# VectorE's score blocks as a fourth concurrent row tile, conversions in pairs, and new planner rules, in an attention kernel with two softmax engines

## The chip, the cores and the metric

The kernel runs on one core of one Trainium2 chip. The metric is the device time of one execution in microseconds (us); lower is better. One execution of each kernel was profiled, the others were timed. Where a ratio is given, it is the mean time of one kernel's fast runs over that of the kernel before in the same rounds on the same chip, so it is not quite the ratio of the medians quoted beside it. "Fast" means within 1.5% of the fastest run of the same kernel; a run above that is called slow.

## The reference

Two independent attention blocks with 2048 positions, 512 channels, 32 heads of 16 channels each; the results lie side by side.

```python
def _A_ref(x, wqkv, wo):        # linear attention, cut
    pq, pk = phi(q), phi(k)     # phi(t) = where(t > 0, t + 1, exp(t)) + 1e-6
    kv = einsum("bhsd,bhse->bhde", pk, v); z = einsum("bhsd->bhd", pk)
    o = einsum("bhqd,bhde->bhqe", pq, kv) / (einsum("bhqd,bhd->bhq", pq, z) + 1e-6)
    return o @ wo
def _B_ref(x, wqkv, wo):        # softmax attention, cut
    p = softmax(einsum("bhqd,bhkd->bhqk", q, k) * 16 ** -0.5)
    return einsum("bhqk,bhkd->bhqd", p, v) @ wo
```

The softmax block dominates: 32 heads of 2048 x 2048 exponentials. The kernel cuts it into 2048 *blocks*, each of 128 keys and 512 queries of one head; 64 blocks (4 heads, all keys, the same 512 queries) make a *unit*.

## The kernel before

ScalarE takes most blocks by its exponential. VectorE takes the rest with an integer trick: one conversion of the scores to int16 out of PSUM (`DI`), then a *chain* of four cheap operations over a group of blocks. TensorE makes the scores (32 rows of the array per block) and multiplies the results with the values.

A planner writes the program: it keeps a clock `T` for each engine, asks each source of work for its next candidate, and takes the earliest. Its estimates only fix the order of instructions; semaphores fix the real times. So **any edit of a rule gives another program**.

The kernel uses eight banks of PSUM: five for ScalarE's scores (fills of 3 and of 2 blocks in turn), one accumulator `PVb` for the value products of one unit, and two spare banks `DB`. VectorE's scores share the spare banks with all other work: projections, the whole linear attention, the output.

```python
ABL = (3, 2); DG = 3; NDG = 5; DNEXT = 16           # fills; blocks per chain group; groups; see fill_d_cand
DI = sb("DI", [128, NDG, DG * 512], I16)
DQ = sb("DQ", [128, 2, DG * 512], I16)              # temporaries of the chain
PVb = ps("pPV", [128, 512], F32)
DB = [ps("pD%d" % i, [128, 512], F32) for i in range(2)]

def qk(e, dst, b):                                  # scores of one block: 32 rows of the array, row group g
    u, j, g = b
    Gp, c, e_ = unit(u)
    return e.matmul(dst, lhsT=KM[32*g:32*g+32, Gp % 2, e_, j*128:(j+1)*128],
                    rhs=QT[32*g:32*g+32, Gp % 2, c*512:(c+1)*512], start=True, stop=True, tile_position=(32*g, 0))

def fill_act_cand():                                # ScalarE's fill: 3 or 2 blocks in different row groups
    ...
    def f(e):
        for i, b in enumerate(bl):
            ins = qk(e, SCR[sl][:, i*512:(i+1)*512], b)
        return ins
    sch.add("pe", f, reads=qk_reads(bl), writes=skeys(sl))

def fill_d_cand():                                  # VectorE's block: a TensorE item of its own
    ...
    elif left[u] < DNEXT:                           # near the end of a unit: take from the next one
        u += 1
    ...
    sch.add("pe", lambda e: qk(e, f32v(bk), bl[0]), reads=qk_reads(bl), writes=[bk[3]])
    ... e.tensor_scalar(DI[:, buf, i*512:(i+1)*512], f32v(bk), ESC, EB, op0=ALU.mult, op1=ALU.add)
```

The value product of a unit must be complete before the next unit may start in `PVb`. ("Head" and "head's end": a unit and its end.)

## Time and profile before

| | before |
|---|---|
| time, median of 4 runs | 879.28 us (876.78 to 881.74) |
| span of the profiled run | 877.5 us |
| blocks on ScalarE / VectorE | 1699 / 349 |
| ScalarE idle between its first and last exponential | 58.2 us |
| of that in stretches over 1 us | 34.8 us in 10 stretches |

The last two rows are counted from the trace (0.2 us more than before the exponentials alone, as some idle time lies before other instructions).

The first parts of the page of the kernel before follow. The first line of numbers has the busy time of each engine. The rows of digits are ScalarE's busy share in tenths in 40 equal slices of the span; PEclk is the clock that TensorE was granted, in tenths of full speed.

```profile
span 877.5 us, 12952 instructions
...
PE 756.4 (86%) x5361; PEld 225.4 (26%) x5406; DVE 733.2 (84%) x1245; ACT 799.5 (91%) x737; POOL 45.9 (5%) x43
...
ACT  6999989999999999999897997999889889999793
...
PEclk9989989999999989878776798978897879687777
```

ScalarE is the busiest engine, and the late slices of PEclk are much lower than the early ones. Next, groups by line and shape of the kernel before: engine, operation, tile written and read, shapes, count, then busy time, mean ns of one, and the idle time of the engine just before them, with what ended it.

```profile
L726 ACT ACTIVATE PT<-pS 128x1536 f16<-128x1536 f32 x340 | 526.2, 1548 | 37.8 <-PE pS L662 36.4 <-PE pD L662 0.6
L726 ACT ACTIVATE PT<-pS 128x1024 f16<-128x1024 f32 x339 | 380.1, 1121 | 20.2 <-PE pS L662 17.8 <-PE pD L662 1.8
L777 DVE TENSOR_SCALAR DI<-pD 128x512 int16<-128x512 f32 x349 | 230.3, 683 | 34.7 <-PE pD L662 26.0 <-PE pS L662 7.1
...
L662 PE MATMUL pD<-QT,KM 32*128 32x512 bf16 x349 | 133.4, 432 | 16.2 <-DVE DI L777 7.9 <-DVE VNa L545 2.7 <-DVE PQT L535 2.1
...
L816 DVE TENSOR_TENSOR DQ<-DQ 128x1536 bf16<-128x1536 int16 x116 | 109.9, 951 | 1.0
```

The exponentials cost 788.0 us together, or 788.0 / 1699 = 0.464 us a block. The 58 us of idle time before them ended almost always with a score matmul: ScalarE starves for scores. A VectorE block costs 0.68 us for the conversion and a third of the chain.

In ten-microsecond windows of the kernel before, three places look like this (busy time and count of each engine, then the granted clock, DMA share and GB/s).

```profile
core 0: us, PE busy (x) PEld busy (x) DVE busy (x) ACT busy (x) POOL busy (x), PEclk, DMA share, GB/s
520.00:530.00 10.00, 6.26 (x28) 2.03 (x29) 9.73 (x16) 4.81 (x5) 1.03 (x1) 0.79 0.00 0
630.00:640.00 10.00, 7.27 (x43) 2.01 (x43) 9.53 (x17) 4.91 (x5) 0.00 (x0) 0.58 0.05 15
810.00:820.00 10.00, 5.32 (x24) 1.61 (x21) 9.51 (x15) 5.33 (x5) 0.00 (x0) 0.50 0.00 0
```

ScalarE loses half of each window and VectorE is the busy one. TensorE pauses, and its granted clock is low there.

### The profile page before, as it was taken

Reading aid. Unit: us, or ns where it says so; the run is one execution under the profiler, and the core shown is the slowest. Engines: PE = TensorE matmul, PEld = TensorE weight load, DVE = VectorE, ACT = ScalarE, POOL = GpSimd, SP = SyncE. Lnnn points to the kernel's source line nnn. Section 1 sums busy time; section 2 is a strip of 40 time slices with the busy share of each in tenths; the row PEclk is TensorE's granted clock in tenths of the full one; section 3 lists DMA queues with packets and bytes.
Section 4 is the critical chain, followed back from the end, with each engine's and each line's share of the span. In section 5 each row is a group of like instructions: output and inputs, shape, how many; then the busy total and the mean of one; then the engine's idle time right before and its main releaser. Section 6 shows DMA issues by size and latency. Waiting matters only on the chain.

```text
span 877.5 us, 12952 instructions
## 1 busy us (share of the span) xinstructions
PE 756.4 (86%) x5361; PEld 225.4 (26%) x5406; DVE 733.2 (84%) x1245; ACT 799.5 (91%) x737; POOL 45.9 (5%) x43
## 2 busy tenths in 40 slices
PE   8989889988888889888988878899689889888776
PEld 5323323223222222212222122222122222221212
DVE  5796665898889978899989999799998998979882
ACT  6999989999999999999897997999889889999793
POOL 2000021100000022100000012200000000000000
PEclk9989989999999989878776798978897879687777
DMA  9001000000000000000000000000000000000000
GB/s 313 24 2 49 1 1 1 1 2 1 1 1 1 1 1 1 1 13 7 7 1 6 8 7 7 1 7 7 6 7 1 7 7 31 7 25 1 7 19 27
DMA packets 13137, 13.48 MB, mean 15 GB/s; under 512 B 1808, under 2 KB 12560, under 8 KB 13072
## 3 DMA queue, kind: packets, MB, share of 16 engines
q1 hardware_dynamic: 12272, 12.19, 4.3%
q8 instruction: 44, 0.72, 0.3%
q10 hardware_dynamic: 800, 0.39, 0.2%
q14 instruction: 21, 0.17, 0.1%
HBM read 8.39 MB, written 4.19 MB: 14 GB/s over the span
## 4 chain that ended last, share of the span: by engine, by line
ACT 55%; PE 24%; DVE 19%; issue 1%; POOL 0%; ACTq 0%; POOLq 0%
ACT PT L726 54%; PE pPV L872 8%; DVE DI L777 7%; PE pS L662 7%; DVE DI L818 3%; DVE DQ L816 3%; PE pD L662 3%; DVE DQ L817 1%; DVE DQ L815 1%; PE pD L896 1%; PE pD L448 1%; ACT EA L532 1%; PE pD L613 1%; PE pD L604 1%; DVE OT L893 1%
## 5 line engine op out<-in xcount | busy, mean ns | idle before, releaser
L726 ACT ACTIVATE PT<-pS 128x1536 f16<-128x1536 f32 (+1 forms) x680 | 788.0, 1334 | 58.0 <-PE pS L662 54.2
L662 PE MATMUL pS<-QT,KM 32*128 32x512 bf16 x1699 | 295.6, 430 | 65.9 <-ACT PT L726 59.9
L777 DVE TENSOR_SCALAR DI<-pD 128x512 int16<-128x512 f32 x349 | 230.3, 683 | 34.7 <-PE pD L662 26.0
L872 PE MATMUL pPV<-PT,VV 128*17 128x512 f16 x1699 | 213.3, 437 | 2.9 <-DVE OT L893 1.7
L662 PE MATMUL pD<-QT,KM 32*128 32x512 bf16 x349 | 133.4, 432 | 16.2 <-DVE DI L777 7.9
L662 PEld LDWEIGHTS pS<-QT,KM 32*128 32x128 bf16 x1699 | 65.3, 92 | 308.0 <-ACT PT L726 260.6
L816 DVE TENSOR_TENSOR DQ<-DQ 128x1536 bf16<-128x1536 int16 (+1 forms) x117 | 110.3, 946 | 1.0
L818 DVE TENSOR_TENSOR DI<-DI,DQ 128x1536 int16<-128x1536 int16 (+1 forms) x117 | 110.0, 946 | 0.9
L872 PE MATMUL pPV<-DI,VV 128*17 128x512 f16 x349 | 86.5, 437 | 10.6 <-DVE DI L818 10.2
L474 POOL TENSOR_SCALAR KM<-KR,PAR 128x512 bf16<-128x512 bf16 x24 | 41.1, 1725 | 519.4 <-DVE KR L472 519.4
L815 DVE TENSOR_SCALAR DQ<-DI 128x1536 int16<-128x1536 int16 (+1 forms) x117 | 64.4, 557 | 0.7
L817 DVE TENSOR_SCALAR DQ<-DQ 128x1536 f16<-128x1536 bf16 (+1 forms) x117 | 64.4, 557 | 0.7
L872 PEld LDWEIGHTS pPV<-PT,VV 128*17 128x17 bf16 x1699 | 37.1, 89 | 91.7 <-issue 77.2
L662 PEld LDWEIGHTS pD<-QT,KM 32*128 32x128 bf16 x349 | 29.7, 93 | 90.0 <-DVE DI L777 41.2
L541 PE MATMUL pD<-Wa,xTa 128*128 128x256 bf16 x256 | 40.5, 288 | 0.9 <-DVE VNa L545 0.4
L448 PE MATMUL pD<-xTb,Wb 128*128 128x512 bf16 x103 | 34.0, 410 | 4.6 <-issue 2.1
L896 PE MATMUL pD<-identf,OT 128*128 128x128 f32 x128 | 30.4, 349 | 4.0 <-DVE OT L893 2.4
L893 DVE COPY OT<-pPV 128x512 f32<-128x512 f32 x32 | 21.9, 685 | 13.4 <-PE pPV L872 13.3
L417 DVE CAST OB<-pD 128x512 bf16<-128x512 f32 x30 | 20.6, 687 | 13.2 <-PE pD L613 13.0
L532 ACT ACTIVATE EA<-pD 128x256 bf16<-128x256 f32 (+1 forms) x48 | 28.0, 584 | 0.7 <-PE pD L541 0.7
L541 PEld LDWEIGHTS pD<-Wa,xTa 128*128 128x128 bf16 x256 | 21.2, 101 | 19.4 <-issue 10.5
L872 PEld LDWEIGHTS pPV<-DI,VV 128*17 128x17 bf16 x349 | 17.0, 91 | 35.3 <-DVE DI L818 17.4
(88 smaller groups left out, 378.9 us busy)
## 6 DMA issues: line engine op xcount, KB each, us to landing
out_dram<-OB SPq DMA_DIRECT2D x32, 128.0 KB, 1.7
KNa<-in_A_x_dram SPq DMA_DIRECT2D x4, 512.0 KB, 6.2
ON<-in_B_x_dram SPq DMA_DIRECT2D x3, 512.0 KB, 7.5
Wa<-in_A_wqkv_dram SPq DMA_DIRECT2D x1, 1536.0 KB, 12.0
Wb<-in_B_wqkv_dram SPq DMA_DIRECT2D x2, 384.0 KB, 8.4
Wb<-in_B_wqkv_dram SPq DMA_DIRECT2D x1, 512.0 KB, 6.6
WOb<-in_B_wo_dram SPq DMA_DIRECT2D x1, 512.0 KB, 12.1
WOa<-in_A_wo_dram SPq DMA_DIRECT2D x1, 512.0 KB, 12.2
```

The costliest lines, as they stand in the source:

```text
L448: return e.matmul(f32v(bk), lhsT=Wb[:, cc, kind * 512 + Gp * 128:kind * 512 + Gp * 128 + 128], rhs=xTb[:, cc, sc * 512:(sc + 1) * 512], st ...
L474: st.append(("pool", 0.7, f_op("pool", lambda e, e_=e_: e.tensor_scalar(KM[:, r, e_, cs], KR[:, kr, :], PAR[:, e_:e_ + 1], None, op0=ALU.m ...
L541: return e.matmul(f32v(bk)[:, 256 * k_:256 * k_ + 256], lhsT=xTa[:, cc, t * 128:(t + 1) * 128], rhs=Wa[:, cc, 512 + 512 * k_ + 256 * hp:51 ...
L662: return e.matmul(dst, lhsT=KM[32 * g:32 * g + 32, Gp % 2, e_, j * 128:(j + 1) * 128], rhs=QT[32 * g:32 * g + 32, Gp % 2, c * 512:(c + 1) ...
L726: sch.add("act", lambda e: e.activation(PT[:, row, c0:c0 + w], SCR[sl][:, 0:w], ACTF.Exp, scale=SC), reads=skeys(sl), writes=[("PT", row, ...
L777: sch.add("dve", lambda e: e.tensor_scalar(DI[:, buf, i * 512:(i + 1) * 512], f32v(bk), ESC, EB, op0=ALU.mult, op1=ALU.add), reads=[bk[3]] ...
L815: (0.07 + w * 0.00027, lambda e: e.tensor_scalar(Dq, I, 0x200, 6, op0=ALU.bitwise_xor, op1=ALU.logical_shift_left), ik, [("DQ", q)]),
L816: (0.07 + w * 0.00053, lambda e: e.tensor_tensor(Dqb, Dq, Dq, op=ALU.mult), [("DQ", q)], [("DQ", q)]),
L817: (0.07 + w * 0.00027, lambda e: e.tensor_scalar(Dqh, Dqb, EC, EO, op0=ALU.mult, op1=ALU.add), [("DQ", q)], [("DQ", q)]),
L818: (0.07 + w * 0.00053, lambda e: e.tensor_tensor(I, I, Dqh, op=ALU.add), ik + [("DQ", q)], ik)]
L872: sch.add("pe", lambda e, g=g, j=j, h=h, P=P, first=first, last_=last_: e.matmul(PVb[32 * g:32 * g + 17, 0:512], lhsT=VV[:, j, vcol(h):vco ...
L896: return e.transpose(f32v(bk)[:, qb * 128:(qb + 1) * 128], OT[:, ob, qb * 128:(qb + 1) * 128], identf[:])
```

## The change

Its intent: a fill of 3 uses three of the four row groups of the array, so a VectorE block can ride along as the fourth, and TensorE no longer spends a separate slot on it. Two VectorE blocks that lie in both spare banks are converted by one operation. Along with it come new rules for the planner.

```diff
-    DG = 3
-    NDG = 5
+    DG = 4
+    NDG = 4
-    DNEXT = 16
+    DNEXT = 24
+    DLEAD = 0.5
+    DBL = 5.0
-        DQ = sb("DQ", [128, 2, DG * 512], I16)
+        DQ = sb("DQ", [128, 1, DG * 512], I16)
-        DB = [ps("pD%d" % i, [128, 512], F32) for i in range(2)]
+        DB = ps("pD", [128, 1024], F32)
 ...
+        def d_pick(at, used):
+            bi = min((i for i in range(2) if dfree[i] is not None), key=lambda i: (dfree[i], i), default=None)
+            u = cur_unit()
+            if bi is None or u is None or dfree[bi] > at or d_backlog(at) > DBL:   # bank free now; backlog under 5 us
+                return None
 ...
+        def d_emit(tk, en):
+            for b, buf, bi, i in tk:
+                bk = DBANK[bi]
+                sch.add("pe", lambda e, bk=bk, b=b: qk(e, f32v(bk), b), reads=qk_reads([b]), writes=[bk[3]])
+            pair = len(tk) == 2 and tk[0][1] == tk[1][1] and tk[0][2] == 0 and tk[1][2] == 1
 ...
+                    sch.add("dve", lambda e: e.tensor_scalar(DI[:, buf, i * 512:(i + n) * 512], DB[:, bi * 512:(bi + n) * 512],
+                                                             ESC, EB, op0=ALU.mult, op1=ALU.add),
 ...  in fill_act_cand:
+                tk = []
+                while len(bl) + len(tk) < 4:
+                    pk = d_pick(st + 0.05, [g for _, _, g in bl] + [x[0][2] for x in tk])
+                    if pk is None:
+                        break
+                    tk.append(d_take(pk))
                 sch.add("pe", f, reads=qk_reads(bl), writes=skeys(sl))
+                if tk:
+                    tk.sort(key=lambda x: x[3])
+                    d_emit(tk, en + 0.05)
 ...  fill_d_cand stays for blocks alone, with the same rules
```

`d_backlog` is VectorE's planned work ahead plus 1 us for each block whose chain has not been scheduled. I call `DBL` the *cap* and `DNEXT` the *head limit*. `DLEAD`: a block alone is planned no earlier than 0.5 us before VectorE's planned work runs out.

More of the change, by code (lines that the diff above doesn't have):

```diff
@@ L296, in bass_concat_heads__linear_attn_block__softmax_full_mha__prompt_kernel @@
         PVb = ps("pPV", [128, 512], F32)
-        DB = [ps("pD%d" % i, [128, 512], F32) for i in range(2)]
+        DB = ps("pD", [128, 1024], F32)
         def bank(T, b0, key):
             return (T, T.bitcast(BF), b0 * 512, key)
-        DBANK = [bank(DB[i], 0, ("D", i)) for i in range(2)]
+        DBANK = [bank(DB, i, ("D", i)) for i in range(2)]
         SBANKS = [bank(SCR[i], b, ("S", i, b)) for i in range(2) for b in range(ABL[i])]
@@ L677, in bass_concat_heads__linear_attn_block__softmax_full_mha__prompt_kernel @@
         ptfree = {}
-        dgroup = {"n": 0, "buf": 0, "items": [], "open": False}
+        dgroup = {"n": 0, "buf": 0, "open": False}
         dgfree = [0.0] * NDG
         dgleft = [0] * NDG
-        qfree, qwait = [0, 1], []
+        qfree, qwait = [0], []
         def cur_unit():
@@ L687, in cur_unit, with d_backlog @@
             return None
+        def d_backlog(at):
+            w = max(0.0, T["dve"] - at) + sum(c_[3] for c_ in cands["dve"])
+            for s_ in dgroup["st"].values():
+                if not s_.get("chained"):
+                    w += 1.0 * len(s_["items"])
+            return w
+        def d_pick(at, used):
[3 more added lines that the diff above has]
+                return None
+            if u == NU - 1:
+                if left[u] < DEND:
+                    return None
+            elif left[u] < DNEXT:
+                u += 1
+            if not dgroup["open"]:
+                buf = dgroup["n"] % NDG
+                if dgfree[buf] is None or dgfree[buf] > at:
+                    return None
+            else:
+                buf = dgroup["buf"]
+            ch = choose(u, 1, used)
+            if ch is None or not ch[0] or ch[1] > at:
+                return None
+            return ch[0][0], buf, bi
@@ new lines, in d_take @@
+        def d_take(pk):
+            b, buf, bi = pk
+            take([b])
+            dfree[bi] = None
+            if not dgroup["open"]:
+                dgroup.update(open=True, buf=buf)
+                dgroup["n"] += 1
+                dgfree[buf] = None
+                dgleft[buf] = 0
+                dgroup["st"][buf] = {"p1": 0, "closed": False, "items": []}
+            s_ = dgroup["st"][buf]
+            i = len(s_["items"])
+            s_["items"].append(b)
+            dgleft[buf] += 1
+            if len(s_["items"]) == DG:
+                s_["closed"] = True
+                dgroup["open"] = False
+            return b, buf, bi, i
@@ new lines, in d_emit, with p1 @@
+        def d_emit(tk, en):
[3 more added lines that the diff above has]
+            pair = len(tk) == 2 and tk[0][1] == tk[1][1] and tk[0][2] == 0 and tk[1][2] == 1
+            for part in ([tk] if pair else [[x] for x in tk]):
+                n = len(part)
+                _, buf, bi, i = part[0]
+                def p1(st_, en_, part=part, n=n, buf=buf, bi=bi, i=i):
+                    sch.add("dve", lambda e: e.tensor_scalar(DI[:, buf, i * 512:(i + n) * 512], DB[:, bi * 512:(bi + n) * 512],
+                                                             ESC, EB, op0=ALU.mult, op1=ALU.add),
+                            reads=[("D", bi + x) for x in range(n)], writes=[("DI", buf, i + x) for x in range(n)])
+                    for x in range(n):
+                        dfree[bi + x] = en_ + LAT
+                    s_ = dgroup["st"][buf]
+                    s_["p1"] += n
+                    s_["t"] = en_
+                    chain(buf)
+                push("dve", en + LAT, 0, 0.1 + 0.55 * n, p1)
@@ L689, in fill_act_cand @@
+        dgroup["st"] = {}
         def fill_act_cand():
@@ L719, in run @@
                 sch.add("pe", f, reads=qk_reads(bl), writes=skeys(sl))
+                if tk:
+                    tk.sort(key=lambda x: x[3])
+                    d_emit(tk, en + 0.05)
+                    T["pe"] = en + 0.05
                 w = 512 * len(bl)
@@ L734, in fill_d_cand @@
         def fill_d_cand():
-            bi = min((i for i in range(2) if dfree[i] is not None), key=lambda i: dfree[i], default=None)
-            if bi is None:
-                return None
-            u = cur_unit()
-            if u is None:
-                return None
-            if u == NU - 1:
-                if left[u] < DEND:
-                    return None
-            elif left[u] < DNEXT:
-                u += 1
-            if not dgroup["open"]:
-                buf = dgroup["n"] % NDG
-                if dgfree[buf] is None:
-                    return None
-                t1 = dgfree[buf]
-            else:
-                buf, t1 = dgroup["buf"], 0.0
@@ L753, in fill_d_cand @@
-            ch = choose(u, 1)
-            if ch is None or not ch[0]:
-                return None
-            bl, t0 = ch
-            start = max(T["pe"], t0, t1, dfree[bi])
-            def run(st, en):
-                take(bl)
-                dfree[bi] = None
-                if not dgroup["open"]:
-                    dgroup.update(open=True, buf=buf, items=[])
-                    dgroup["n"] += 1
-                    dgfree[buf] = None
-                    dgleft[buf] = 0
-                i = len(dgroup["items"])
-                items = dgroup["items"]
-                items.append(bl[0])
-                dgleft[buf] += 1
-                state = dgroup.setdefault("st", {})
-                state.setdefault(buf, {"p1": 0, "closed": False})
-                if i == 0:
-                    state[buf] = {"p1": 0, "closed": False, "items": items}
-                bk = DBANK[bi]
-                sch.add("pe", lambda e: qk(e, f32v(bk), bl[0]), reads=qk_reads(bl), writes=[bk[3]])
-                def p1(st_, en_):
-                    sch.add("dve", lambda e: e.tensor_scalar(DI[:, buf, i * 512:(i + 1) * 512], f32v(bk), ESC, EB, op0=ALU.mult, op1=ALU.add),
-                            reads=[bk[3]], writes=[("DI", buf, i)])
-                    dfree[bi] = en_ + LAT
-                    state[buf]["p1"] += 1
-                    state[buf]["t"] = en_
-                    chain(buf)
-                push("dve", en + LAT, 0, 0.62, p1)
-                if len(items) == DG:
-                    state[buf]["closed"] = True
-                    dgroup["open"] = False
@@ L787, in fill_d_cand @@
-            return start, 0.3, run
+            fr = [x for x in dfree if x is not None]
+            if not fr:
+                return None
+            busy = max(T["dve"], T["pe"]) if not cands["dve"] else max(T["dve"], T["pe"]) + sum(c_[3] for c_ in cands["dve"] if c_[0] < T["dve"] + 1.0)
+            at = max(T["pe"], min(fr), busy - DLEAD)
+            if dgroup["open"] is False and dgfree[dgroup["n"] % NDG] is not None:
+                at = max(at, dgfree[dgroup["n"] % NDG])
+            at = max(at, T["pe"] + d_backlog(T["pe"]) - DBL + 0.01)
@@ L789, in close_group @@
+            pk = d_pick(at + 1e-6, ())
+            if pk is None:
+                return None
+            def run(st, en):
+                tk = [d_take(pk)]
+                pk2 = d_pick(st + 0.05, [tk[0][0][2]])
+                if pk2 is not None:
+                    tk.append(d_take(pk2))
+                tk.sort(key=lambda x: x[3])
+                d_emit(tk, en)
+            return at, 0.32, run
         def close_group():
@@ L798, in chain @@
                 return
+            s_["chained"] = True
             qwait.append(buf)
@@ L1083, in bass_concat_heads__linear_attn_block__softmax_full_mha__prompt_kernel @@
             S=S, NT=NT, NC=NC, vcol=vcol, xTb=xTb, Wb=Wb, WOb=WOb, VV=VV, QT=QT, KM=KM, PT=PT, ON=ON, OT=OT, ZR=ZR, ONT=ONT, OB=OB,
-            identb=identb, identf=identf, BMk=BMk, SCR=SCR, PVb=PVb, MB=DB[0], GM=OT[:, 0, 0:2 * NT].rearrange("p (a t) -> p a t", a=2), GT=RD[0:NT, 0, :], out=out), gsems)
+            identb=identb, identf=identf, BMk=BMk, SCR=SCR, PVb=PVb, MB=DB, GM=OT[:, 0, 0:2 * NT].rearrange("p (a t) -> p a t", a=2), GT=RD[0:NT, 0, :], out=out), gsems)
         totals = {}
```

## The prediction

> **What bounds it now.** By the page's first part, ScalarE is busy 799.5 us of 877.5 (91%), TensorE 756.4, VectorE 733.2. By the groups by form, ScalarE's exponentials are 340 of 3 blocks (1548 ns each) and 339 of 2 (1121 ns): 788.0 us for 1699 of the 2048 score blocks, 0.464 us a block. VectorE does the other 349. In the chain of waits ScalarE holds 55%, TensorE 24%, VectorE 19%: ScalarE sets the pace, but is starved. Idle before the exponentials is 58.0 us, 54.2 of it for the score matmuls. The timeline around 470-480 us shows a typical loss: value matmuls wait 1.4 us for a late VectorE block of a head (the single accumulator bank can't go on to the next head), TensorE's granted clock is 0.60, and ScalarE is busy 5.6 of 10 us. In ten-microsecond windows the same happens at 520, 630, 710 and 810 us (ScalarE 4.8, 4.9, 6.3, 5.3). Another 10 us at the start and 14 at the end have none.
>
> **What changes.**
> 1. TensorE. The 349 VectorE score matmuls often run alone (timeline, 466-472 us), with ScalarE's next fill behind them in order. The Trainium skill (TensorE: Matmul & The Clock Gate, Packing small matmuls) says matmuls in different row groups overlap; this trace agrees: bursts of 2 or 3 take the 0.39 us of one. As fourth tile (or third and fourth beside a two-block fill) a block should cost almost nothing. Estimate: about 0.2 us for each of some 250-300 blocks, 50-60 us of TensorE time, not all critical.
> 2. VectorE. A 512-wide conversion takes 683 ns. The skill (VectorE: DVE Perf Modes, errata table) gives PSUM-source time as a constant plus one cycle per element at 0.96 GHz, so estimate 533 ns + 150 fixed, and 1216 ns for 1024: 75 ns saved per block of a pair. The trace confirms 683 only. The chain's four operations per three blocks take 559+951+559+951 = 3020 ns; for four I estimate 3.8 us, 0.95 against 1.01 a block. Together 1.69 to about 1.56-1.60: 30-45 us.
> 3. The planner can give VectorE more blocks: I expect 370-410 instead of 349, 10-28 us less ScalarE work (0.464 each).
> 4. VectorE blocks go to the next head from 24 blocks left, not 16, and VectorE's backlog is capped at 5 us. Both should make the late VectorE block at a head's end rarer.
> 5. Against: a pair takes both spare banks at once, which projections and output jobs share; the groups of four close later; one temporary instead of two; fewer separate matmuls may let the granted clock (0.866) fall.
>
> **Sum.** Exponentials about 770 (1660 blocks), other ScalarE 11 in the main stretch, start and end 26, leaving idle: 58 now, perhaps 35-40 after. That is about 845.
>
> **Predicted:** 847 us, 8 in 10 between 825 and 873. Faster by over 2%: 0.74; within 2%: 0.20; slower: 0.06.
>
> **Signs.** The conversion group shows 1024-wide forms near 1.2 us, most blocks in pairs; score matmuls to the VectorE banks start within nanoseconds of a fill's, with less waiting for VectorE before them; idle before the exponentials under 45 us; exponential blocks below 1680; TensorE busy under 720 us.
>
> **What would make it wrong.** If the idle before exponentials does not fall, the stalls are from latency at a head's end or the clock, not TensorE work. If VectorE's blocks fall below 340, the cap bites and ScalarE gains work. If pairs are rare, the VectorE gain is missing. If jobs starve for banks, the end without exponentials grows.

## More of the kernel before

Where does it starve? This timeline of the kernel before (start, length, engine, line, operation; idle time and its end in brackets) shows the costliest kind of place, a head's end.

```profile
632.14 0.68 DVE L777 TENSOR_SCALAR DI<-pD 128x512 int16<-128x512 f32 x1
...
633.61 0.95 DVE L818 TENSOR_TENSOR DI<-DI,DQ 128x1536 int16<-128x1536 int16 x1
634.61 0.60 PE L872 MATMUL pPV<-DI,VV 128*17 128x512 f16 x3 [2.40 <-DVE DI L818]
...
635.41 0.68 DVE L893 COPY OT<-pPV 128x512 f32<-128x512 f32 x1
...
638.46 0.60 PE L662 MATMUL pS<-QT,KM 32*128 32x512 bf16 x5
...
638.90 1.45 ACT L726 ACTIVATE PT<-pS 128x1536 f16<-128x1536 f32 x1 [5.09 <-PE pS L662]
```

A VectorE block of the old head is converted at 632.14; its chain ends after 634.5; the value matmuls on `DI` have waited 2.40 us for it; only then can the accumulator be copied (L893) and the value products and scores of the next head follow. ScalarE had sat idle for 5.09 us at 638.90.

The clock records of the trace say which came first: at this place the clock fell to half at 628.2 us and ScalarE's wait began at 633.8, and all ten stretches over 1 us begin while the clock is already at half. So the late VectorE block need not be the only cause of such a stall; a slow TensorE may be another.

## The result

| | before | after |
|---|---|---|
| time, median of 4 runs | 879.28 us | 832.85 us (828.85 to 834.93) |
| ratio of fast runs, 95% interval | | 0.9467 (0.9414 to 0.9519) |
| span of the profiled run | 877.5 us | 833.1 us |
| blocks on ScalarE / VectorE | 1699 / 349 | 1682 / 366 |
| ScalarE idle between its first and last exponential | 58.2 us | 23.2 us |
| of that in stretches over 1 us | 34.8 us (10) | 7.3 us (3) |
| VectorE blocks whose score matmul starts within 60 ns of one of a fill | 116 of 349 | 326 of 366 |

The last three rows are counted in the traces. The page of the kernel after, the same parts:

```profile
span 833.1 us, 12897 instructions
...
PE 695.8 (84%) x5406; PEld 210.7 (25%) x5406; DVE 748.5 (90%) x1153; ACT 789.1 (95%) x730; POOL 46.5 (6%) x43
...
ACT  5799999999999999999999999999999999999993
...
PEclk9999999999999799998786999999988998699996
```

TensorE is busy 60.6 us less (the trace of before misses 45 of its 5406 matmuls, none of them scores; and part of the fall comes with the clock, as VectorE's score matmuls went from 432 to 415 ns on average), VectorE 15 us more, and ScalarE's share rises from 91% to 95%. The granted clock is 0.924 on average, against 0.866. The groups of the kernel after that answer to those above:

```profile
L810 ACT ACTIVATE PT<-pS 128x1536 f16<-128x1536 f32 x336 | 536.4, 1596 | 14.6 <-PE pS L664 8.3 <-PE pD L664 5.1
L810 ACT ACTIVATE PT<-pS 128x1024 f16<-128x1024 f32 x337 | 394.9, 1172 | 8.4 <-PE pD L664 6.1 <-PE pS L664 2.1
...
L750 DVE TENSOR_SCALAR DI<-pD 128x512 int16<-128x512 f32 x348 | 234.0, 682 | 29.3 <-PE pD L664 27.2 <-PE pS L664 0.3
L664 PE MATMUL pD<-QT,KM 32*128 32x512 bf16 x366 | 142.6, 415 | 1.3 <-DVE DI L750 1.1
...
L867 DVE TENSOR_TENSOR DQ<-DQ 128x2048 bf16<-128x2048 int16 x91 | 111.1, 1221 | 1.5
...
L750 DVE TENSOR_SCALAR DI<-pD 128x1024 int16<-128x1024 f32 x9 | 10.9, 1213 | 3.3 <-PE pD L664 3.3
```

Three things to see. The idle time before the exponentials is 14.6 + 8.4 us. The exponentials did not become slower, though their means are about 50 ns higher: instructions that follow each other without a pause overlap in the trace (536.4 + 394.9 is more than the 778.7 us in which any of them ran), and 778.7 / 1682 is 0.463 us a block, as before. And only 9 of the 357 conversions are 1024 wide (the last line): a pair needs both spare banks free at once, and the plan rarely has that. The same three windows, in the kernel after:

```profile
520.00:530.00 10.00, 8.15 (x60) 2.45 (x59) 8.53 (x15) 8.70 (x9) 2.24 (x2) 0.83 0.00 0
630.00:640.00 10.00, 8.78 (x70) 2.31 (x67) 9.90 (x15) 9.62 (x9) 0.00 (x0) 0.91 0.05 16
810.00:820.00 10.00, 7.05 (x38) 1.90 (x38) 1.41 (x4) 6.84 (x7) 0.00 (x0) 0.63 0.04 13
```

ScalarE is now 87% and 96% busy in the first two, though these are other places of the program by now; the last is where the exponentials end.

The fourth tile itself is seen best in TensorE's timelines. First the kernel before, where scores for `pD` (VectorE) and `pS` (ScalarE) take turns:

```profile
466.30 0.39 PE L662 MATMUL pS<-QT,KM 32*128 32x512 bf16 x3
466.98 0.39 PE L662 MATMUL pD<-QT,KM 32*128 32x512 bf16 x1 [0.29 <-DVE DI L777]
467.22 0.39 PE L662 MATMUL pS<-QT,KM 32*128 32x512 bf16 x2
467.58 0.45 PE L662 MATMUL pD<-QT,KM 32*128 32x512 bf16 x1
```

and the kernel after, where the block for `pD` starts 0.01 us after the fill:

```profile
404.06 0.39 PE L664 MATMUL pS<-QT,KM 32*128 32x512 bf16 x3
404.07 0.39 PE L664 MATMUL pD<-QT,KM 32*128 32x512 bf16 x1
404.50 0.39 PE L664 MATMUL pS<-QT,KM 32*128 32x512 bf16 x2
404.51 0.38 PE L664 MATMUL pD<-QT,KM 32*128 32x512 bf16 x1
```

**The sum.** Between first and last exponential, ScalarE's idle time fell by 35.0 us (58.2 to 23.2), its busy time in all by 10.4 us (799.5 to 789.1), and the stretch after the last exponential grew by 1.1 us (15.2 to 16.3). That is 44.3 of the 44.4 us of span. So most of the gain is an end to starving, not less work. The clock records split it further: 51.2 of the 58.2 us of idle time before, and 16.2 of the 23.2 us after, lie where TensorE had half its clock (a score matmul takes 0.60 us there and 0.39 us at full clock). Between the first and the last exponential that was 228.7 us before and 116.8 us after. ScalarE starves mostly at half clock; there is half as much of it now, and a smaller share of it is idle (22% before, 14% after). No run holds the clock fixed, so whether the better clock is a cause of the gain or an effect is not shown. The experiments ask what ended the starving.

### The profile page after: what moved, and what is told of

Same layout as the page of the kernel before. It is cut to its first block, busy times and chain, and to the rows that moved or that the text cites. A ratio compares the mean times of both kernels' runs of the same rounds, so it can differ in the third digit from the quotient of the medians.

```text
span 833.1 us, 12897 instructions
## 1 busy us (share of the span) xinstructions
PE 695.8 (84%) x5406; PEld 210.7 (25%) x5406; DVE 748.5 (90%) x1153; ACT 789.1 (95%) x730; POOL 46.5 (6%) x43
## 4 chain that ended last, share of the span: by engine, by line
ACT 69%; PE 16%; DVE 14%; issue 1%; POOL 0%; POOLq 0%
ACT PT L810 67%; PE pS L664 5%; PE pPV L923 5%; DVE DI L750 4%; DVE DQ L867 2%; DVE DI L869 2%; ACT EA L534 1%; DVE DQ L866 1%; PE pD L450 1%; PE pD L947 1%; DVE DQ L868 1%; PE pD L615 1%; DVE OT L944 1%; PE pD L543 1%; PE pD L970 0%
## 5 line engine op out<-in xcount | busy, mean ns | idle before, releaser
L810 ACT ACTIVATE PT<-pS 128x1536 f16<-128x1536 f32 (+1 forms) x673 | 778.7, 1384 | 23.1 <-PE pD L664 11.2
L664 PE MATMUL pS<-QT,KM 32*128 32x512 bf16 x1682 | 277.5, 410 | 104.3 <-ACT PT L810 100.0
L750 DVE TENSOR_SCALAR DI<-pD 128x512 int16<-128x512 f32 (+1 forms) x357 | 244.9, 695 | 32.6 <-PE pD L664 30.6
L923 PE MATMUL pPV<-PT,VV 128*17 128x512 f16 x1682 | 220.9, 410 | 0.7 <-ACT PT L810 0.3
L664 PE MATMUL pD<-QT,KM 32*128 32x512 bf16 x366 | 142.6, 415 | 1.3 <-DVE DI L750 1.1
L869 DVE TENSOR_TENSOR DI<-DI,DQ 128x2048 int16<-128x2048 int16 x92 | 112.0, 1217 | 1.6
L867 DVE TENSOR_TENSOR DQ<-DQ 128x2048 bf16<-128x2048 int16 x92 | 111.8, 1215 | 1.5
L923 PE MATMUL pPV<-DI,VV 128*17 128x512 f16 x366 | 79.7, 425 | 3.0 <-DVE OT L944 2.4
L866 DVE TENSOR_SCALAR DQ<-DI 128x2048 int16<-128x2048 int16 x92 | 64.0, 696 | 1.8
L868 DVE TENSOR_SCALAR DQ<-DQ 128x2048 f16<-128x2048 bf16 x92 | 62.8, 683 | 0.4
L923 PEld LDWEIGHTS pPV<-DI,VV 128*17 128x17 bf16 x366 | 16.3, 90 | 28.5 <-issue 12.5
```

Source lines behind the costliest of these rows:

```text
L664: return e.matmul(dst, lhsT=KM[32 * g:32 * g + 32, Gp % 2, e_, j * 128:(j + 1) * 128], rhs=QT[32 * g:32 * g + 32, Gp % 2, c * 512:(c + 1) ...
L750: sch.add("dve", lambda e: e.tensor_scalar(DI[:, buf, i * 512:(i + n) * 512], DB[:, bi * 512:(bi + n) * 512], ESC, EB, op0=ALU.mult, op1=A ...
L810: sch.add("act", lambda e: e.activation(PT[:, row, c0:c0 + w], SCR[sl][:, 0:w], ACTF.Exp, scale=SC), reads=skeys(sl), writes=[("PT", row, ...
L866: (0.07 + w * 0.00027, lambda e: e.tensor_scalar(Dq, I, 0x200, 6, op0=ALU.bitwise_xor, op1=ALU.logical_shift_left), ik, [("DQ", q)]),
L867: (0.07 + w * 0.00053, lambda e: e.tensor_tensor(Dqb, Dq, Dq, op=ALU.mult), [("DQ", q)], [("DQ", q)]),
L868: (0.07 + w * 0.00027, lambda e: e.tensor_scalar(Dqh, Dqb, EC, EO, op0=ALU.mult, op1=ALU.add), [("DQ", q)], [("DQ", q)]),
```

## The experiments

The rivals. *Theory A*: TensorE's time; the row tiles overlap, so fills come sooner. *Theory B*: the planner's new rules (cap and head limit) end the stalls at a head's end. *Theory C*: order; a VectorE block that waits for its bank no longer stands in front of a fill.

The median of before was 880.35, 880.15 and 878.57 us in the three batches.

### e1: the fourth block in an occupied row group

```diff
-        def d_emit(tk, en):
+        def d_emit(tk, en, row=None):
-                sch.add("pe", lambda e, bk=bk, b=b: qk(e, f32v(bk), b), ...
+                sch.add("pe", lambda e, bk=bk, b=(b if row is None else (b[0], b[1], row)): qk(e, f32v(bk), b), ...
-                    d_emit(tk, en + 0.05)
+                    d_emit(tk, en + 0.05, bl[-1][2])
```

The order of instructions was compared with the kernel after and is the same on every engine.

> The kernel after, with one thing changed: a VectorE block that is issued with a ScalarE fill uses the row group of the fill's last block instead of its own free one, so it cannot overlap with it. Order, counts, waits and every other instruction are the same on all engines; the output is wrong on purpose. Theory A (the gain is TensorE time: the fourth tile costs nothing): most of the gain goes, 855 to 880 us, ratio to before 0.97 to 1.0, idle before the exponentials back over 45 us. Theory B (the gain is the new rules of the planner, which keep a late VectorE block from stalling a head's end): 835 to 847 us, ratio 0.95 to 0.965, few idle stretches over 1 us.

Measured: 884.91 (the profiled run), 845.66, 862.02 and 861.91 us. The lower the mean granted clock of the run, the longer it took: 0.85, 0.917, 0.887 and 0.878 (the last two all but equal in time). Three of the four runs count as slow by the 1.5% rule (of the 75 runs of the other kernels in the three batches one did, so the spread belongs to e1), so there is no ratio of fast runs; the one fast run is 845.66 / 880.35 = 0.961 of before, the kernel after 0.944 to 0.947. (The wrong scores passed the comparison with the reference: computed from the inputs, the scores have a standard deviation of 0.003, so nearly every exponential is 1.) The profile shows that the edit did what it should. The kernel of e1, its exponentials and TensorE:

```profile
L810 ACT ACTIVATE PT<-pS 128x1536 f16<-128x1536 f32 (+1 forms) x673 | 785.3, 1331 | 66.0 <-PE pS L664 61.7
...
226.07 0.39 PE L664 MATMUL pS<-QT,KM 32*128 32x512 bf16 x3 [0.64 <-ACT PT L810]
226.30 0.37 PE L664 MATMUL pD<-QT,KM 32*128 32x512 bf16 x1
```

The fourth block starts 0.23 us after the fill, not 0.01. Only 27 of 366 VectorE blocks now start with a fill (326 after). In this slow run the idle time before the exponentials is 66.0 us, as Theory A expected, and 30.9 us of it lie in 22 stretches over 1 us, where Theory B expected few. What the lost overlap can cost is seen in windows of e1's profiled, slow run:

```profile
500.00:550.00 50.00, 45.70 (x332) 12.05 (x327) 47.95 (x73) 49.85 (x47) 5.15 (x3) 1.00 0.03 9
750.00:800.00 50.00, 50.00 (x227) 10.39 (x219) 32.83 (x49) 34.73 (x29) 0.00 (x0) 0.50 0.03 11
```

and of a second profile of the kernel after (e9 below):

```profile
500.00:550.00 50.00, 42.67 (x338) 12.10 (x336) 48.31 (x73) 50.00 (x48) 10.10 (x6) 1.00 0.02 6
750.00:800.00 50.00, 42.64 (x350) 12.47 (x346) 47.25 (x74) 50.00 (x46) 0.00 (x0) 1.00 0.06 19
```

At full clock, 500 to 550 us, e1 keeps ScalarE as busy as the kernel after: TensorE, busy 45.7 of 50 us, still has room. From about 731 us on TensorE got half its clock for 95.6 us, the longest such stretch in the trace (13.7 us in the kernel after); with 50.00 of 50 us busy it then bounds the kernel, and ScalarE does 34.7 us of work.

What follows: with everything else equal, the overlap is worth 1.5% by e1's one fast run (845.66 against 832.85 us; 1.9% against e9's 829.82). Its slow runs would make it three fifths of the gain (862 us) or all of it (885 us), but a slow run is not a fair partner for a fast one, so these are not counted. The fast run lies inside Theory B's band, the other three in Theory A's or beyond. The profile is of a slow run: it shows how more can be lost, not how often. There too the loss lies at half clock (59.1 of the 65.6 us that ScalarE is idle between its first and last exponential), and why TensorE was granted half its clock for so long in that run is not shown. So A holds for a part, of which 1.5% is shown.

### e2: no cap on VectorE's backlog

```diff
-    DBL = 5.0
+    DBL = 1000.0
```

> The kernel after without the cap of 5 us on VectorE's backlog (406 VectorE blocks planned, 366 in the kernel after). Theory A: the fourth tile still works and ScalarE has 40 blocks less (18 us), so 815 to 835 us, ratio 0.93 to 0.95. Theory B: the long idle stretches of ScalarE at the ends of heads come back (over 1 us: 7.3 us in sum after, 34.8 before; expected over 30), 850 to 880 us, ratio 0.965 to 1.0.

Measured: 909.57 us, ratio 1.0333 (1.0287 to 1.038), slower than before. Both theories missed. VectorE took 406 blocks, and the last exponential ended earlier than in the kernel after, near 808 us of 908.5; but 100.6 us of other work came after it (16.3 after). Windows of e2:

```profile
750.00:808.00 58.00, 46.83 (x350) 11.94 (x348) 55.18 (x79) 55.68 (x49) 0.00 (x0) 0.88 0.03 10
808.00:858.00 50.00, 31.25 (x180) 13.56 (x180) 30.32 (x61) 7.16 (x12) 0.00 (x0) 0.90 0.09 32
858.00:908.00 50.00, 29.27 (x144) 12.40 (x144) 20.36 (x37) 2.39 (x4) 0.00 (x0) 0.58 0.07 23
```

In the last 100 us ScalarE is nearly idle, and VectorE is busy 61% of the first half and 41% of the second. The instructions there are the end of the linear attention (query projections, numerators, transposes and output products). What follows: the cap does not mainly prevent stalls (idle stretches over 1 us rose to 20.8 us only, under the 30 that B expected); by the place of the loss, it leaves spare banks and VectorE time for the side work. Beside a fill a VectorE block is planned with a fill's priority, ahead of all side work.

### e3: the old head limit

```diff
-    DNEXT = 24
+    DNEXT = 16
```

> The kernel after with VectorE's blocks taken from the next head from 16 blocks left, as before, instead of 24 (375 VectorE blocks planned). Theory A: 828 to 838 us, ratio 0.94 to 0.955. Theory B: late blocks again, long idle stretches over 15 us in sum, 842 to 860 us, ratio 0.96 to 0.98.

Measured: 830.61 us, ratio 0.9445 (0.9402 to 0.9488): the same as the kernel after, with 375 blocks on VectorE. Idle stretches over 1 us were 15.7 us, as B expected, but the time was A's. On balance the head limit is worth nothing in this kernel: with nine blocks fewer ScalarE is busy 5.6 us less, and it is idle 2.6 us longer.

### e4: no pairs, a new plan

```diff
-            pair = len(tk) == 2 and ...
+            pair = False and len(tk) == 2 and ...
```

> The kernel after with every VectorE conversion 512 wide, no pairs (367 VectorE blocks planned, 366 with pairs). The profile after shows only 9 pairs, worth 9 times about 150 ns or 1.4 us of VectorE's time, so both theories expect the same time within 0.5%: 829 to 837 us, ratio 0.942 to 0.951. If it is slower by over 1%, the pairs matter through something other than their number.

Measured: 825.31 us, ratio 0.9392 (0.9339 to 0.9445). The expectation missed by half a per cent, on the fast side. The planner makes another plan here (367 VectorE blocks), so e10 repeats this with the plan kept.

### e5: the fourth block in front of the fill

```diff
-                sch.add("pe", f, reads=qk_reads(bl), writes=skeys(sl))
                 if tk:
                     tk.sort(key=lambda x: x[3])
                     d_emit(tk, en + 0.05)
                     T["pe"] = en + 0.05
+                sch.add("pe", f, reads=qk_reads(bl), writes=skeys(sl))
```

The order on VectorE is the same as in the kernel after; TensorE has the same matmuls.

> The kernel after with the same plan, the same counts and the same work on every engine, but each VectorE block that goes with a ScalarE fill stands in front of the fill in TensorE's order, not behind it. It can still overlap with it. Theory C (part of the gain is order: in the kernel before a VectorE block that waits for its bank stands in front of a fill 214 times and holds ScalarE up): slower than after by 1 to 3%, 842 to 862 us, with idle before the exponentials up by 10 us or more and the waits of the VectorE score matmuls for VectorE's conversions back (1.1 us after, 7.9 before, for the matmuls alone). Theory A (only that the rows overlap): within 1% of after, 828 to 841 us.

Measured: 831.70 us, ratio 0.9444 (0.9369 to 0.9519), the same as after. Groups of e5:

```profile
L810 ACT ACTIVATE PT<-pS 128x1536 f16<-128x1536 f32 (+1 forms) x673 | 779.0, 1375 | 23.4 <-PE pS L664 22.4
...
L664 PE MATMUL pD<-QT,KM 32*128 32x512 bf16 x366 | 142.4, 413 | 15.2 <-DVE DI L750 11.6
```

The waits of VectorE's score matmuls came back (11.6 us), the idle time before the exponentials did not (23.4 us). Theory C falls: in this plan, where a block is only taken when its bank is expected to be free, order is worth nothing. But the edit did more than change the order: a block in front no longer waits for its fill, only 203 of the 366 blocks now start within 60 ns of one of a fill (326 after), and TensorE is busy 722.1 us (695.8 after). So e5 also says that 123 overlaps and 26 us of TensorE's busy time can be lost for nothing while the clock stays where it was (0.926); the number of overlaps alone does not measure their worth.

### e6: the new rules in the kernel before

```diff
-    DNEXT = 16
+    DNEXT = 24
+    DBL = 5.0
 ...  in fill_d_cand, with d_backlog as in the kernel after:
-            start = max(T["pe"], t0, t1, dfree[bi])
+            start = max(T["pe"], t0, t1, dfree[bi], T["pe"] + d_backlog(T["pe"]) - DBL + 0.01)
```

> The kernel before with two of the new rules of the planner alone: the cap of 5 us on VectorE's backlog, and VectorE's blocks from the next head from 24 left (333 VectorE blocks planned, 349 before). No fourth tile. Theory A: no gain, 872 to 895 us, ratio 0.99 to 1.02. Theory B (the rules keep late VectorE blocks away): the idle stretches over 1 us fall from 34.8 us in sum to under 15, 855 to 868 us, ratio 0.97 to 0.985.

Measured: 859.76 us, ratio 0.9772 (0.9689 to 0.9854), with 333 blocks on VectorE: faster than before, but not clearly by 2%. Idle stretches over 1 us: 14.9 us in sum (34.8 before). The group of exponentials of e6:

```profile
L734 ACT ACTIVATE PT<-pS 128x1536 f16<-128x1536 f32 (+1 forms) x686 | 796.1, 1361 | 37.6 <-PE pS L663 31.3
```

This is B's number: without any fourth tile two fifths of the gain are there, by fewer stalls, and against 16 more blocks on ScalarE.

### e12: the cap alone in the kernel before

The same edit without the line `DNEXT`.

> The kernel before with the cap on VectorE's backlog alone, and the next head from 16 blocks left as it was (341 VectorE blocks planned). If the cap is what gave 2.3% with both rules: 855 to 866 us, ratio 0.97 to 0.985, idle stretches over 1 us below 20 us in sum. If the head limit gave it: within 1% of before, 872 to 888 us.

Measured: 877.64 us, ratio 0.9989 (0.9941 to 1.0037), with 341 blocks on VectorE; stretches over 1 us: 32.1 us. The same group of e12:

```profile
L734 ACT ACTIVATE PT<-pS 128x1024 f16<-128x1024 f32 (+1 forms) x683 | 791.9, 1370 | 49.0 <-PE pS L663 42.7
```

So the cap alone gives nothing. In the kernel before, the head limit is what e6 needs beside it or instead of it; the head limit alone was not run, and one plan of each kind cannot tell a rule from a lucky plan.

### e7: no blocks beside a fill

```diff
-                while len(bl) + len(tk) < 4:
+                while False:
```

> The kernel after without blocks beside a fill: VectorE's blocks get their own place in TensorE's order, alone or in pairs, by the planner's other rule, everything else as after. The plan then has 278 VectorE blocks (366 after), 88 more for ScalarE, which is about 40 us of ScalarE at 0.464 us a block. Theory A: 865 to 895 us, ratio 0.98 to 1.015. Theory B: 840 to 862 us, ratio 0.955 to 0.98.

Measured: 903.57 us, ratio 1.0307 (1.0202 to 1.0412). VectorE gets 278 blocks and is busy 71%; ScalarE has 832.7 us of work (789.1 after) and TensorE 777.0 (695.8). This is past A's band, and not clean: 88 blocks changed sides. It shows only that, with these rules, the planner makes a worse plan when it may put nothing beside a fill.

### e8: groups of four in the kernel before

```diff
-    DG = 3
-    NDG = 5
+    DG = 4
+    NDG = 4
-        DQ = sb("DQ", [128, 2, DG * 512], I16)
+        DQ = sb("DQ", [128, 1, DG * 512], I16)
```

> The kernel before with groups of four in the chain and one temporary in place of groups of three and two (359 VectorE blocks planned, 349 before). The chain costs 3.8 us for four by the trace after, 3.0 for three: 0.95 against 1.01 us a block, about 20 us of VectorE's time in all. If VectorE's time bounded the kernel before, 860 to 872 us, ratio 0.975 to 0.99; if it did not, within 1% of before, 872 to 888 us.

Measured: 923.18 us, ratio 1.0496 (1.0416 to 1.0575). Both expectations missed: it is the slowest kernel of all. The group of exponentials of e8:

```profile
L726 ACT ACTIVATE PT<-pS 128x1536 f16<-128x1536 f32 (+1 forms) x676 | 782.6, 1344 | 74.3 <-PE pS L662 64.5
```

Idle stretches over 1 us are 57.0 us, and 45.6 us follow the last exponential (15.2 before). That VectorE work was cheaper per block (by the groups of before and after, 0.96 us of chain in place of 1.0) did not matter. A group that must collect four blocks finishes its first one later, which fits the stalls; but the plan changed as a whole, and I have not separated the two.

### e9 and e10: the kernel after again, and its pairs split

e9 is the kernel after without an edit. e10 keeps its plan and writes each pair as two conversions:

```diff
-                    sch.add("dve", lambda e: e.tensor_scalar(DI[:, buf, i * 512:(i + n) * 512], DB[:, bi * 512:(bi + n) * 512], ...
+                    for y in range(n):
+                        sch.add("dve", lambda e, y=y: e.tensor_scalar(DI[:, buf, (i + y) * 512:(i + y + 1) * 512], DB[:, (bi + y) * 512:(bi + y + 1) * 512], ...
```

> The kernel after, unchanged, as the mark for the other three of this chip: 828 to 836 us, ratio to before 0.941 to 0.952.

> The kernel after with its plan kept instruction for instruction, but each of the nine 1024-wide conversions written as two 512-wide ones. Theory: pairs are too rare to matter (9 x 150 ns, 1.4 us at most), so within 0.4% of the run of after beside it, and the 1% gain of the run with no pairs came from another plan. If pairs cost something (both banks held longer), 822 to 828 us, as in that run.

Measured, five rounds each: e9 829.82 us, ratio 0.9436 (0.9393 to 0.9479); e10 827.42 us, ratio 0.9418 (0.9382 to 0.9454). The result fits both of the expected ranges (within 0.4% of e9, and just under 828 us), and the two intervals overlap: no difference is seen. The second half of the change's name, conversion in pairs, is worth nothing here, because it happens nine times.

### e11: groups of three, no pairs

e4's edit, and `DG = 3`, `NDG = 5` and two temporaries as in the kernel before.

> The fourth tile and the cap, without pairs, and with the chain's groups of three and two temporaries of the kernel before (389 VectorE blocks planned, 366 after). If groups of four were of use: slower than after, 835 to 850 us. If groups of three wait less to fill, as the loss of groups of four in the kernel before suggests: 818 to 828 us, with 23 blocks less on ScalarE (11 us).

Measured: 875.00 us, ratio 0.9947 (0.9911 to 0.9982). This missed by far, and the windows of e11 say where the time went:

```profile
750.00:798.00 48.00, 40.92 (x293) 10.47 (x289) 43.96 (x73) 46.35 (x42) 0.00 (x0) 0.82 0.04 12
798.00:836.00 38.00, 25.14 (x147) 11.41 (x146) 19.65 (x36) 4.96 (x9) 0.00 (x0) 0.81 0.09 32
836.00:874.00 38.00, 23.08 (x100) 9.21 (x100) 15.06 (x28) 2.39 (x4) 0.00 (x0) 0.59 0.08 27
```

The exponentials ended at 798 us, earlier than in the kernel after, with only 4.2 us of idle stretches over 1 us. But 76.3 us followed. It looks like e2's loss, at 389 VectorE blocks: the side work was pushed to the end. Neither it nor any other run clearly beats the kernel after; e4's and e10's intervals overlap with it.

## Why the prediction was right, and where it was not

The time, 832.85 us, lies within the stated 825 to 873, and "faster by over 2%" had the chance 0.74. The parts:

1. **What bounds it** (ScalarE, starved of scores): right. 35.0 of the 44.4 us of span are idle time of ScalarE that went away.
2. **TensorE, step 1**: right in kind. The fourth block starts 0.01 us after the fill; 326 of 366 blocks overlap. But 116 of 349 already did, so about 210 blocks gained, not 250 to 300; at 0.23 us (e1) that is some 48 us, an estimate. TensorE's busy time fell 60.6 us. e1's fast run shows directly that taking the overlap away costs 1.5%.
3. **VectorE, step 2**: wrong. "Together 1.69 to about 1.56-1.60: 30-45 us" took pairs to be the rule. The estimate for one was good (1216 ns expected, 1213 measured), but there were 9. Conversion and chain went from (230.3 + 349.1) / 349 = 1.66 us a block to (244.9 + 350.6) / 366 = 1.63, which is 12 us in all, and e10 shows that pairs add nothing.
4. **More blocks for VectorE, step 3**: 366, just under 370 to 410. The exponentials took 778.7 us and not 770.
5. **The planner's rules, step 4**: half right. Together they remove stalls (e6: 2.3% in the kernel before). But I took the head limit and the cap for two cures of the same stall. In the kernel after the head limit does nothing (e3), and without the cap the kernel is slower than before, since side work is left to the end (e2). I had named starved jobs only as a risk of pairs; the fourth tile's priority brings it, and the cap holds it off.
6. **The clock, step 5**: it rose to 0.924 and did not fall.

The size that was off in the sum is the idle time left: 35-40 us in the prediction, 23 measured (19.5 in e9), and this outweighs the 9 us missing in step 4. "Other ScalarE 11 in the main stretch" was too large as well: it was 5.9 us before and 4.8 after, as the other half lies at the start and the end. These errors have opposite signs, so the time came out nearer to 847 us than its parts did, and that is luck.

What stays open: how the gain divides between overlap and rules. e1's fast run puts the overlap at 1.5% of the 5 to 6%, and its slow runs cannot be counted; e6 puts the rules at 2.3% alone. Something is left over. From e6 to the kernel after, the span falls by 26.8 us: 17.1 us are less ScalarE work between the first and last exponential (33 blocks fewer), 13.9 us less idle time, and the start and the end grow by 4.2 us. So a part of the gain may be that the fourth tile lets the planner give VectorE more blocks (e7, without it, has 278); e1 keeps the plan and cannot show that part. Also open are whether the head limit alone would do what e6 did, and what the better clock does by itself: the idle time sits at half clock in before, after and e1 alike, and no run separates the clock from the pauses of TensorE.

## What to carry to other kernels

When the engine that bounds the kernel starves, give the engine that feeds it slack: a matmul with few rows that rides beside another one can cost it next to no time (its start came 0.01 us after the fill's here), and here the granted clock was higher as well. Split the idle time by the granted clock before you name its cause. Work that rides along inherits the priority of what carries it, so it needs a cap, or it crowds out the side work and the loss appears at the end of the program: look at the stretch after the last bottleneck instruction as well as at its idle time. And check how often a merged operation can happen (both banks free at once) before counting what one saves.

## What the Trainium skill lacked or had wrong

- "TensorE: Matmul & The Clock Gate", Part 1: the page has full clock return after one busy window of some 3.4 us. In e1's profiled run the clock stayed at half for 95.6 us while the profile has TensorE busy 50.00 of 50 us in it (matmul ends are modelled, and 182 of the 438 matmuls there are scores of 32 rows). The same part warns that the clock's trace events have been unreliable, and that the clock has been seen stuck at a quarter for over 50 us; here the matmuls bear the half clock out (a score matmul took 604 ns in those 50 us). The page's other finding, that these events hold half and full clock alone, agrees: the traces of before, after and e1 hold the values 0.5 and 1.0 alone.
- The same page, Part 3 (packing): a few ns between the starts of row tiles. This agrees (0.01 us between the first of three blocks and the fourth; 0.23 us when the row group is taken). The page does not say that a lack of overlap may cost nothing at full clock and show only when the clock falls, as in e1's windows (ScalarE busy 49.85 of 50 us at full clock, 34.73 at half).
- "VectorE: DVE Perf Modes", errata table: 120 cycles plus one per element for a PSUM source, which is 658 ns for 512 and 1192 for 1024 elements. Measured: 682 and 1213 ns, so the slope agrees ((1213 - 682) / 512 = 1.04 ns) and the fixed part is about 150 ns, not 125.
- No page says what a plan loses when filler work takes the priority of the work that it fills: 100.6 us after the last exponential (e2), against 16.3.
